# A quarter of one MLP weight chunk in each attention step: 32-row slices of a long PSUM sum in the idle row group

## The chip, the cores and the metric

One NeuronCore of one Trainium2 chip runs the whole program. The metric is the device time of that core in microseconds (us), the median of several executions. All executions that are compared here are fast, at a granted TensorE clock of 1.0 (0.998 in two executions).

Part of the scatter is the start of the program, which is the same in all versions: the 101st matmul with w1 starts between 28.60 and 29.19 us in the 14 profiles. Where a small difference matters, the text also gives the time from the start of that matmul to the end of the last matmul, called "without the start".

The engines have short names in the profile: PE is TensorE's matmuls, PEld its weight loads, DVE is VectorE, ACT is ScalarE, POOL is GpSimd, and SPq is the DMA queue that SyncE feeds. "Bank" is one of the eight parts in which the program uses PSUM; each holds the 512 float32 output columns of one matmul. An evacuation is the copy of finished results out of a bank, which frees the bank.

## The reference, cut to what matters

```python
x = A_x                                  # 2048 tokens x 1024
xn = layernorm(x)
return x + A(xn, wq, wk, wv, wo, beta) + B(xn, w1, b1, w2, b2)

# A: attention, 32 heads of 32, in 4 segments of 512 tokens: causal softmax
#    inside a segment, a linear-attention memory M, z over earlier segments
logits = einsum('bhqd,bhkd->bhqk', q_s, k_s) * scale + mask   # contraction over 32
p = softmax(logits); a_dot = p @ v_s; ...; o @ wo
# B: an MLP over the token axis, 3584 hidden units
u = gelu(einsum('bsd,sf->bdf', layernorm(xn), w1) + b1)
y = einsum('bdf,fs->bds', u, w2) + b2    # contraction over 3584 = 28 chunks of 128
```

Two kinds of work matter here. The logits contract over only 32 rows, so four heads share the 128-row array as four row groups: in the trace of the kernel before, the first four matmuls of a step in different row groups start 3 to 7 ns apart. The second MLP product contracts over 3584 rows: 32 output tiles (16 token chunks, two halves of 512 columns), each a sum of 28 full matmuls; 24 of them also add 8 matmuls of `o @ wo` to the same sum.

## The kernel before

The program is emitted by a small list scheduler. It emits attention tasks in order ("crit"), and between them it emits single matmuls of MLP output sums ("fill"), so that PE always has something to do. A logits step is one task. It takes seven banks: in a first round each of the four row groups streams 512 columns, in a second round three of them do. In the second round one row group, the "short" one, rotates with the step and has nothing to do.

```python
# _Kernel.step: items are (row group r, blocks); seven of them, four first
def mms(*bs):
    for i, u, r, kb, col in jobs:
        self.fw.mm(self.ps[:, bs[i], col:col + SEG_L - kb * P],
                   self.kT[u % 3][32*r:32*r+32, kb*P:(kb+1)*P],
                   self.qT[u % 3][32*r:32*r+32, kb*P:SEG_L],
                   start=True, stop=True, tile_position=(32*r, 0))
box = fl.pe(mms, reads, banks=len(slots), wall=True, ns=637)

# _Fill.step: one matmul of the current sum; the sum's bank stays taken meanwhile
st, sp = at == 0, at == size - 1
with fw.group(reads=reads, writes=[k.R_bank[b]] if st or sp else []):
    if at < N_FCH:                                     # 28 chunks of w2
        w, _ = k.w2_ring.get(4 * j + at // 7)          # 6 slots of 7 chunks
        fw.mm(k.bank(b), w[:, at % 7, :], k.gT[:, at, half*512:(half+1)*512],
              start=st, stop=sp)
    else:                                              # o @ wo, 8 more
        ...
# ... [cut: loads, projections, weighing, evacuation, the tail]
```

The two halves of a token chunk follow each other and use the same w2 slots, so each w2 chunk is loaded once.

## Time and profile before

| | before |
|---|---|
| time | 692.94 us (692.87 to 693.18) |
| PE busy | 687.3 of 691.2 us |
| 128-row matmuls with w2 | 896 |
| logits steps | 46, median 550.5 ns (541 to 559) |
| PE waits after the first 12 us | none |
| DMA moved | 77 MB, engines 44% busy |

A step's length is read from the single matmul records of the trace, from the start of its first matmul to the start of the next 128-row matmul. The page of the kernel before has these lines: busy time by engine, the DMA queue, the chain that ended last, the group of w2 matmuls (busy us, mean ns of one, idle before), and its loads (KB each, median us from issue to landing).

```profile
PE 687.3 (99%) x4822; PEld 329.7 (48%) x4822; DVE 260.3 (38%) x600; ACT 283.9 (41%) x516; POOL 145.1 (21%) x379
...
q1 hardware_dynamic: 211290, 76.59, 44.1%
...
PE 98%; ACT 1%; DMA 0%; DVE 0%; POOL 0%; issue 0%; SPq 0%; DVEq 0%
...
L217 PE MATMUL ps_all<-gT,w2h 128*128 128x512 bf16 x896 | 228.5, 379 | 0.0
...
w2h<-in_B_w_dram SPq DMA_DIRECT2D x64, 224.0 KB, 3.3
```

PE is the chain. A busy PE alone would not prove it, since the records of matmuls overlap: one lasts 379 ns (its end is modelled), while the records start 216 ns apart. So the next question is whether PE ever waits. The view of who PE waited for has one line:

```profile
PE ps_all L217 <- DVE gT L760: 1.3, 1, 1.3
```

That is the start of the program. The third view is one step in the timeline of PE (start us, us, then what ran):

```profile
411.64 0.38 PE L217 MATMUL ps_all<-gT,w2h 128*128 128x512 bf16 x1
411.96 0.61 PE L217 MATMUL ps_all<-qT,kT 32*128 32x512 bf16 x10
412.50 0.39 PE L217 MATMUL ps_all<-gT,w2h 128*128 128x512 bf16 x1
```

From 411.96 to 412.50 is the step. The last 128-row matmul started at 411.64, 0.32 us earlier instead of 0.216: about 0.1 us is lost on the way into the step. The trace shows 96 ns before each of the 46 steps (95 or 96 in all of them); what the engine does in that time is not shown.

### The profile page before, as it was taken

What the parts mean: (1) busy time and instruction counts of PE and PEld (TensorE: products, weight loads), DVE (VectorE), ACT (ScalarE), POOL (GpSimd) and SP (SyncE); (2) the same over time, 40 slices, a digit from 0 to 9 for tenths busy, and PEclk for the clock granted to TensorE, in tenths of its full rate; (3) what the DMA queues carried; (4) which work ended last, traced back from release to release, by engine and by line L of the source; (5) the groups of instructions that cost most, each with busy time, mean ns of one, the idle gap of its engine ahead of it and who ended that gap; (6) DMA issues with size and microseconds to landing.
All of it is one profiled execution on the core that took longest, in us unless ns stands there. A gap on an engine that the chain in (4) does not pass through costs nothing.

```text
span 691.2 us, 11771 instructions
## 1 busy us (share of the span) xinstructions
PE 687.3 (99%) x4822; PEld 329.7 (48%) x4822; DVE 260.3 (38%) x600; ACT 283.9 (41%) x516; POOL 145.1 (21%) x379
## 2 busy tenths in 40 slices
PE   9999999999999999999999999999999999999998
PEld 3444444444444544454454544444445444454454
DVE  6731100000002343344554564554545454353444
ACT  7331111111135455555455344455543435436420
POOL 5820000000001222223132122223221313214310
PEclk9999999999999999999999999999999999999999
DMA  8377666323027355444443526444452525242232
GB/s 309 119 180 183 155 157 206 94 61 101 1 102 194 69 120 133 103 117 114 101 113 75 128 46 131 96 104 102 99 128 60 111 62 123 68 108 70 52 99 83
DMA packets 211343, 77.33 MB, mean 112 GB/s; under 512 B 173915, under 2 KB 203611, under 8 KB 211291
## 3 DMA queue, kind: packets, MB, share of 16 engines
q1 hardware_dynamic: 211290, 76.59, 44.1%
q8 instruction: 38, 0.62, 0.4%
q14 instruction: 15, 0.11, 0.1%
HBM read 59.79 MB, written 5.24 MB: 94 GB/s over the span
## 4 chain that ended last, share of the span: by engine, by line
PE 98%; ACT 1%; DMA 0%; DVE 0%; POOL 0%; issue 0%; SPq 0%; DVEq 0%
PE ps_all L217 98%; ACT xn_tmp L809 0%; DMA xin<-in_A_x_dram 0%; ACT xn_tmp L811 0%; DVE h L850 0%; POOL ln_r L842 0%; SPq L245 0%; DVE fin L1292 0%; POOL ln_t L840 0%; DVE ln_mv L825 0%; DVEq L65 0%
## 5 line engine op out<-in xcount | busy, mean ns | idle before, releaser
L217 PE MATMUL ps_all<-gT,w2h 128*128 128x512 bf16 x896 | 228.5, 379 | 0.0
L1098 POOL TENSOR_SCALAR_AFFINE_SELECT pT<-pT 128x256 bf16<-128x256 bf16 (+1 forms) x320 | 118.8, 373 | 506.8 <-ACT pT L1090 493.9
L1090 ACT ACTIVATE pT<-ps_all 128x512 bf16<-128x512 f32 x320 | 161.8, 620 | 142.4 <-PE ps_all L217 142.2
L217 PE MATMUL ps_all<-h,w1all 128*128 128x512 bf16 x896 | 193.9, 379 | 0.2
L217 PEld LDWEIGHTS ps_all<-h,w1all 128*128 128x128 bf16 x896 | 87.5, 98 | 106.4 <-issue 0.8
L217 PEld LDWEIGHTS ps_all<-gT,w2h 128*128 128x128 bf16 x896 | 79.8, 97 | 85.2 <-issue 10.3
L964 ACT ACTIVATE gT<-ps_all,bc 128x512 bf16<-128x512 f32 x56 | 37.7, 689 | 140.6 <-PE ps_all L217 140.6
L1140 DVE CAST ost<-ps_all 128x264 bf16<-128x264 f32 (+1 forms) x128 | 50.0, 395 | 76.0 <-PE ps_all L217 75.8
L217 PEld LDWEIGHTS ps_all<-vA,pT 128*128 128x128 bf16 x1280 | 50.2, 96 | 28.8
L217 PE MATMUL ps_all<-xnT,wq 128*128 128x512 bf16 x256 | 60.5, 379 | 0.0
L217 PE MATMUL ps_all<-xnT,wk 128*128 128x512 bf16 x256 | 60.5, 379 | 0.0
L217 PE MATMUL ps_all<-wv_sb,xnT 128*128 128x512 bf16 x256 | 60.1, 379 | 0.0
L217 PE MATMUL ps_all<-vA,pT 128*128 128x33 bf16 x1280 | 51.5, 178 | 0.0
L902 DVE TENSOR_SCALAR gcol<-gcol 128x32 f32<-128x32 f32 x1 | 0.2, 183 | 118.7 <-ACT gcol L900 118.7
L217 PEld LDWEIGHTS ps_all<-wv_sb,xnT 128*128 128x128 bf16 x256 | 25.1, 98 | 30.2
L217 PEld LDWEIGHTS ps_all<-xnT,wk 128*128 128x128 bf16 x256 | 25.1, 98 | 30.2
L217 PEld LDWEIGHTS ps_all<-xnT,wq 128*128 128x128 bf16 x256 | 25.1, 98 | 30.2
L975 DVE TENSOR_SCALAR etmp<-etmp 128x512 bf16<-128x512 bf16 x48 | 14.1, 294 | 61.3 <-ACT etmp L974 61.3
L991 DVE CAST vA<-ps_all 128x512 bf16<-128x512 f32 x20 | 13.9, 694 | 56.7 <-PE ps_all L217 54.2
L217 PE MATMUL ps_all<-wo_sb,oT 128*128 128x512 bf16 x128 | 33.1, 379 | 0.0
L990 ACT ACTIVATE kT<-ps_all 128x512 bf16<-128x512 f32 x32 | 19.1, 597 | 34.1 <-PE ps_all L217 34.1
L991 DVE CAST qT<-ps_all 128x512 bf16<-128x512 f32 x20 | 13.8, 692 | 46.1 <-PE ps_all L217 46.1
(69 smaller groups left out, 427.2 us busy)
## 6 DMA issues: line engine op xcount, KB each, us to landing
w2h<-in_B_w_dram SPq DMA_DIRECT2D x64, 224.0 KB, 3.3
w1all<-in_B_w_dram SPq DMA_DIRECT2D x12, 1024.0 KB, 5.2
wq<-in_A_wq_dram SPq DMA_DIRECT2D x32, 256.0 KB, 3.0
wk<-in_A_wk_dram SPq DMA_DIRECT2D x32, 256.0 KB, 3.0
stg<-in_A_x_dram SPq DMA_DIRECT2D x16, 256.0 KB, 3.1
out_dram<-stg SPq DMA_DIRECT2D x16, 256.0 KB, 2.2
xin<-in_A_x_dram SPq DMA_DIRECT2D x5, 512.0 KB, 6.7
wv_sb<-in_A_wv_dram SPq DMA_DIRECT2D x2, 1024.0 KB, 8.3
```

What stands on the lines that cost most here:

```text
L217: ins = self.nc.tensor.matmul(out, *args, **kwargs)
L902: fw.op("dve", lambda e: e.tensor_scalar(self.gcol[:], self.gcol[:], 1.0, None, op0=ALU.add), reads=[self.R_gcol], writes=[self.R_gcol])
L964: fw.op("act", lambda e: e.activation(self.gT[:, fc, half * 512:(half + 1) * 512], self.bank(b), ACT.Gelu_apprx_tanh, bias=self.b1c[:, fc: ...
L975: fl.op({"dve": (lambda e: e.tensor_scalar(et[:], et[:], 1.0, None, op0=ALU.min), 294, 330)}, [R_et], [R_et], prio=2)
L990: self.flow.op({"act": (lambda e, b: e.activation(dst, view(self.bank(b)), ACT.Copy), 635, 560), "dve": (lambda e, b: e.tensor_copy(dst, v ...
L991: "dve": (lambda e, b: e.tensor_copy(dst, view(self.bank(b))), 690, 727)},
L1090: fl.op({"act": (lambda e, b, slot=slot: e.activation(pT[:, slot, :], self.bank(b), ACT.Exp, scale=SCALE), 620, 530)}, [], [R[slot]], box= ...
L1098: fl.op({"pool": (lambda e, ap=ap, pat=pat: e.affine_select(ap, ap, pattern=pat, compare_op=ALU.is_ge, fill=0.0, base=0, channel_multiplie ...
L1140: fl.op({"dve": (lambda e, b: e.tensor_copy(dst, self.ps[:, b, 0:n * VW]), 150 + n * 35, 185 + n * 35)}, [], [self.R_ost[o][qb]], box=box, ...
```

## The change

The intent: use the idle row group. A sum with 28 chunks needs 28 full matmuls of 216 ns. If its last chunk is cut into four slices of 32 rows, each slice is a matmul of 32 rows by 512 columns, and one of them fits into the idle row group of one step. The rotation of the idle group over four steps covers all four slices. The sum must then stay open over four steps, and its bank is the eighth: the other seven belong to the step. So all other sums must have ended before a step.

This costs more than one edit: two streams of sums ("L" for long ones, "N" for the ordinary ones) instead of one, each with its own weight slots; a step in two parts, the first of which needs four banks and the second the rest; and evacuations of attention results that may go to ACT as well as DVE. Eight of the nine long sums are cut. The core of the diff (the scheduler's pacing, buffer names and semaphore counts are cut):

```diff
@@ _Kernel.step
-        def mms(*bs):
-            for i, u, r, kb, col in jobs:
+        n = fl.stage - 1
+        rs = (3 - n) % 4                      # the short row group of this step
+        def mms(bs, some):
+            for i, u, r, kb, col in some:
                 ...
+        def second(bs, some):
+            if n >= fill.PLAIN and fill.L.sliced():
+                fill.L.cut(rs)
+            mms(bs, some)
+        def parts(bs):
+            k = min(4, len(bs))
+            one = sorted([j for j in jobs if j[0] < k], key=lambda j: j[4])
+            two = sorted([j for j in jobs if j[0] >= k], key=lambda j: j[4])
+            ...                               # two groups, each waits for its own banks
-        box = fl.pe(mms, reads, banks=len(slots), wall=True, ns=637)
+        box = fl.pe(None, reads, banks=len(slots), wall=True, parts=parts)
@@ _Kernel.weigh
-        fl.op({"dve": (... tensor_copy ...)},
+        fl.op({"dve": (... tensor_copy ...),
+               "act": (... activation Copy ...)},
@@ weights
-        self.w2r = [e.take(f"w2h{i}", [P, 7, P], BF16) for i in range(6)]
+        self.w2r = [e.take(f"w2n{i}", [P, 4, P], BF16) for i in range(6)]
+        self.w2l = [e.take(f"w2l{i}", [P, 6, P], BF16) for i in range(3)]
+        self.w2s = [e.take(f"w2s{i}", [P, P], BF16) for i in range(2)]
@@ _Stream
+    def cut(self, r):
+        k.fw.mm(k.bank(self.bank), k.w2s[self.i % 2][32*r:32*r+32, :],
+                k.gT[32*r:32*r+32, N_FCH - 1, half*512:(half+1)*512],
+                start=False, stop=False, tile_position=(32*r, 0))
@@ _Fill
+    PLAIN = 12                                # the first 12 steps carry no slice
+        self.L = _Stream(k, self, long, "L", k.w2l, k.R_w2l, 2, [3])
+        self.N = _Stream(k, self, rest, "N", k.w2r, k.R_w2, 4, [0, 1, 2])  # 4 slots ahead
+    def ready(self, t):                       # may this step start?
+        ...
+        return L.i == self.want(n) and L.open() and not self.N.open()
@@ _Flow.run
+    r = max([r, bs[-1]] if t.parts is None else [r, bs[3], bs[-1] - self.PART])
```

The two halves of a token chunk are now often in different sums or apart in time, so each half loads its own weights.

## The prediction

> **What bounds the kernel now.** TensorE. The busy table gives PE 687.3 of 691.2 us, the chain of waits puts 98% on PE, and the view of who waited for whom lists one PE wait (1.3 us, at the start). In the timeline a 128x512 matmul follows the last one after 216 ns; gaps above the ideal outside the logits steps sum to under 4 us, mostly the warm-up matmuls. The granted clock is 1.0. Only fewer or cheaper PE slots can help; ACT (284 us), DVE (260) and the DMA engines (44%) have room.
>
> A logits step (46 of them, 7 banks, 32-row matmuls in four row groups) takes about 550 ns from its first matmul to the next 128-row one, plus 96 ns lost just before it, against 0.43 us of streaming in two rounds of 512 columns. In the second round one row group is idle. [...]
>
> **What the change does.** By the instruction order, w2 matmuls of 128 rows fall from 896 to 888, and 32 matmuls of 32 rows by 512 columns are added, one in the second round of each of 32 steps, in the idle row group. Every other matmul count and the number of steps are equal.
> - Removed: 8 x 216 ns = 1.73 us of PE time, all on the critical path.
> - Added inside steps: 32 starts at 3 to 7 ns, 0.1 to 0.2 us. A slice is as long as the other columns of that round and should not lengthen it.
> - Loads: each half of an output chunk now loads its own weights, 206 loads of mostly 128 KB instead of 64 of 224 KB, about 14 MB more (77 to 91 MB). In 256-byte packets (18.4 ns each, 16 engines) that is about 65 us of DMA time: 44% becomes about 53%.
> - Prefetch of the ordinary sums: four slots of four matmuls, 16 x 216 ns = 3.5 us ahead. A weight load lands in 3.3 us (median), 4.2 us (90th percentile), and a transpose on the same queue holds the issue for 1.2 us. When such a sum runs 20 or more matmuls in one stretch, the fifth slot can come late. The order shows some six to ten such stretches; I estimate 0.3 to 1.2 us in all.
> - The long stream's sum holds the eighth bank through a step, so ordinary sums must have been evacuated (0.75 us DVE) before it. 56 of 128 attention evacuations go to ACT, which relieves this: 0 to 0.3 us.
>
> **Predicted time.** -1.73 + 0.15 + about 0.6 = -1.0 us: 691.9 us, 691.0 to 693.8 for 8 times in 10. Faster by over 2%: 0.004; within 2%: 0.99; slower: 0.006.
>
> **What would show it.** (1) Steps with a slice, timed from start to next 128-row matmul, still 540 to 565 ns; a serialised slice would add 100 to 200 ns each (3 to 6 us). (2) w2 groups count 888, 1.7 us less streaming. (3) New PE idle time, if any, released by DMA on the short weight tiles between 330 and 650 us; none by ACT or DVE over 0.3 us. (4) DMA share 52 to 55%.
>
> **What would make it wrong.** Slower: late weight loads at more places than I think, as loads collide on a busier queue; a slice that waits at the second round's start, or a second half whose banks come late. Faster than 691: no late loads and a shorter tail.

## The result, and the profile after

| | before | after |
|---|---|---|
| time, first comparison (6 runs each) | 692.95 us | 692.64 us (692.16 to 692.97) |
| time, second comparison (9 and 5 runs) | 692.94 us | 692.38 us (692.19 to 692.76) |
| ratio | | 0.9995 [0.9982, 1.0007], then 0.9991 [0.9979, 1.0004] |
| span of the profiled run | 691.2 us | 690.6 us |
| profiled run without the start | 660.00 us | 659.32 us, 659.44 in run 1 |
| steps, median | 550.5 ns | 545 ns, with or without a slice |
| DMA | 77 MB, 44% | 92 MB, 53.5% |

Ratios here are the mean time of one kernel's fast runs over the mean of the other's fast runs of the same rounds, so they are not quite the ratio of the medians quoted. By the medians the change is worth 0.3 to 0.6 us of 693. Both intervals include 1, so the times alone do not show a gain; the two profiles do, with 0.69 and 0.56 us without the start. Eight removed matmuls alone are 1.73 us. The question is where the other microsecond went.

The page after, with the lines that answer to those before:

```profile
PE 685.7 (99%) x4846; PEld 328.2 (48%) x4846; DVE 241.2 (35%) x545; ACT 299.7 (43%) x571; POOL 152.8 (22%) x379
...
q1 hardware_dynamic: 275642, 91.28, 53.5%
...
PE 97%; ACT 1%; DMA 1%; POOL 0%; DVE 0%; issue 0%; SPq 0%; POOLq 0%; DVEq 0%
...
L217 PE MATMUL ps_all<-gT,w2n 128*128 128x512 bf16 x644 | 151.3, 379 | 0.2 <-DMA w2n<-in_B_w_dram 0.2
...
L217 PE MATMUL ps_all<-gT,w2l 128*128 128x512 bf16 x244 | 63.7, 380 | 0.0
...
w2n<-in_B_w_dram SPq DMA_DIRECT2D x161, 128.0 KB, 2.8
```

644 + 244 = 888 matmuls of 128 rows, eight fewer. The slices are a group of their own in the list by shapes:

```profile
L217 PE MATMUL ps_all<-gT,w2s 32*128 32x512 bf16 x32 | 12.0, 374 | 0.0
```

PE waits, by whom (us in all, times, longest):

```profile
PE ps_all L217 <- DVE gT L800: 1.3, 1, 1.3
PE ps_all L217 <- DVE h L890: 0.7, 2, 0.5
PE ps_all L217 <- DMA w2n<-in_B_w_dram: 0.2, 1, 0.2
```

The first two are the start of the program (the second is missing in the next profile of the same kernel, that of run 1). The third is new. This view counts idle time only after the modelled end of the last matmul, which comes about 160 ns after the next one could have started (379 less 216), so it hides short waits. The distance between matmul starts shows them all. A step with a slice, in the timeline of PE:

```profile
397.32 0.38 PE L217 MATMUL ps_all<-wo_sb,oT 128*128 128x512 bf16 x1
397.63 0.39 PE L217 MATMUL ps_all<-qT,kT 32*128 32x384 bf16 x5
397.86 0.37 PE L217 MATMUL ps_all<-gT,w2s 32*128 32x512 bf16 x1
397.86 0.38 PE L217 MATMUL ps_all<-qT,kT 32*128 32x384 bf16 x6
398.18 0.39 PE L217 MATMUL ps_all<-wo_sb,oT 128*128 128x512 bf16 x1
```

The slice starts with the second round at 397.86, and the next 128-row matmul starts 0.55 us after the step's first: as long as a step without one.

I listed every start-to-start distance between 128-row matmuls after the first 15 us that was over 30 ns longer than the matmul needs, and every step that was too long. Before: none. After, in the first profile: six, 1.23 us in all. Three are late weight loads of ordinary sums (62 ns at 428 us, 377 ns at 602, 143 ns at 627: 0.58 us). Three are other waits (0.65 us). Here is a late load in the PE timeline, from the second profile of the changed kernel:

```profile
598.13 4.48 PE L217 MATMUL ps_all<-gT,w2n 128*128 128x512 bf16 x20
603.12 0.39 PE L217 MATMUL ps_all<-gT,w2n 128*128 128x512 bf16 x1 [0.51 <-DMA w2n<-in_B_w_dram]
```

Twenty matmuls are five slots of four. They run 216 ns apart, so the 21st could have started at 598.13 + 4.32 = 602.45 us. It starts at 603.12, 0.67 us late. By the code its slot is asked for when the sum is at its fifth matmul, 16 x 216 ns = 3.5 us ahead. In this trace the load was issued at 599.14 and landed 3.9 us later, at 603.07. In the first profile all three late loads are those of a sum's 21st matmul, and they landed 4.2, 3.6 and 3.8 us after their issue. Loads of 128 KB land in 2.8 us in the median and in up to 5.0 us.

The other three waits, each in the same place in every profile of this schedule, are in the unfiltered timeline of the first profile. At 368 us a step's second part waits for a bank that DVE (the update of the memory M) frees late:

```profile
368.33 0.29 DVE L1209 TENSOR_TENSOR MZ<-MZ,ps_all 128x132 f32<-128x132 f32 x1 [0.43 <-PE ps_all L217]
...
368.38 0.40 PE L217 MATMUL ps_all<-qT,kT 32*128 32x512 bf16 x4
...
368.77 0.37 PE L217 MATMUL ps_all<-gT,w2s 32*128 32x512 bf16 x1
```

The second round should have begun at 368.60 and began at 368.77. (The slice's own weights are a rival for this wait. The last load of such a weight before it was issued at 352.70 us, and the slowest of these loads in the profile took 2.4 us; the landing of this one is not in the trace.) At 444 us a projection waits for the first bank that ACT frees after a step. All eight banks were taken, seven by the step and one by the long sum that had just ended, which DVE starts to evacuate at 444.98:

```profile
444.25 1.09 ACT L1149 ACTIVATE pT<-ps_all 128x512 bf16<-128x512 f32 x2 [1.73 <-PE ps_all L217]
...
444.34 0.60 PE L217 MATMUL ps_all<-wo_sb,oT 128*128 128x512 bf16 x2
...
444.99 0.38 PE L217 MATMUL ps_all<-xnT,wq 128*128 128x512 bf16 x1
```

Two matmuls from 444.34 on end their streaming at 444.78. The first of the two ACT operations ends at 444.84, and the next matmul starts at 444.99. And at 671 us PE waits for a causal mask on POOL:

```profile
670.01 2.33 POOL L1157 TENSOR_SCALAR_AFFINE_SELECT pT<-pT 128x256 bf16<-128x256 bf16 x4
...
670.90 1.03 PE L217 MATMUL ps_all<-wo_sb,oT 128*128 128x512 bf16 x4
...
672.02 0.17 PEld L217 LDWEIGHTS ps_all<-vA,pT 128*128 128x128 bf16 x4 [0.60 <-POOL pT L1157]
```

The third of these four masks ends at 671.97, and the matmul that needs it starts at 672.03.

The balance of the first profile, from the end of the last matmul before (688.82 us) to after (688.15 us), a gain of 0.67 us:

| term | us |
|---|---|
| eight 128-row matmuls fewer, 8 x 216 ns | -1.73 |
| steps shorter, all 46 (25.33 to 25.26 us with the 0.18 below in it) | -0.24 |
| late w2 loads of ordinary sums, three | +0.58 |
| bank freed late by DVE (0.18) and by ACT (0.20), mask on POOL (0.27) | +0.65 |
| sum | -0.74 |

The sum is within 0.07 us of the gain. A balance of one trace is still only a reading, so its terms were tried on the chip. The exceptions are the mask at 671 us, which no run removes, and the waits at 368 and 444 us, which no run changes alone.

### The profile page after: what moved, and what is told of

Same layout as the page of the kernel before. It is cut to its first block, busy times and chain, and to the rows that moved or that the text cites. A ratio compares the mean times of both kernels' runs of the same rounds, so it can differ in the third digit from the quotient of the medians.

```text
span 690.6 us, 12093 instructions
## 1 busy us (share of the span) xinstructions
PE 685.7 (99%) x4846; PEld 328.2 (48%) x4846; DVE 241.2 (35%) x545; ACT 299.7 (43%) x571; POOL 152.8 (22%) x379
## 3 DMA queue, kind: packets, MB, share of 16 engines
q1 hardware_dynamic: 275642, 91.28, 53.5%
## 4 chain that ended last, share of the span: by engine, by line
PE 97%; ACT 1%; DMA 1%; POOL 0%; DVE 0%; issue 0%; SPq 0%; POOLq 0%; DVEq 0%
PE ps_all L217 97%; DMA w2n<-in_B_w_dram 1%; ACT xn_tmp L849 0%; DMA xin<-in_A_x_dram 0%; ACT xn_tmp L851 0%; POOL pT L1157 0%; DVE h L890 0%; ACT pT L1149 0%; POOL ln_r L882 0%; SPq L247 0%; POOLq L580 0%; DVE fin L1342 0%; POOL ln_t L880 0%; DVE ln_mv L865 0%; DVEq L65 0%
## 5 line engine op out<-in xcount | busy, mean ns | idle before, releaser
L1157 POOL TENSOR_SCALAR_AFFINE_SELECT pT<-pT 128x256 bf16<-128x256 bf16 (+1 forms) x320 | 126.4, 403 | 507.7 <-ACT pT L1149 497.5
L217 PE MATMUL ps_all<-gT,w2n 128*128 128x512 bf16 x644 | 151.3, 379 | 0.2 <-DMA w2n<-in_B_w_dram 0.2
L217 PEld LDWEIGHTS ps_all<-gT,w2n 128*128 128x128 bf16 x644 | 59.6, 98 | 68.4 <-issue 3.1
L217 PE MATMUL ps_all<-gT,w2l 128*128 128x512 bf16 x244 | 63.7, 380 | 0.0
L1462 DVE SCALAR_TENSOR_TENSOR stg<-ps_all,bc,stg 128x512 bf16<-128x512 f32 x32 | 24.0, 750 | 99.2 <-PE ps_all L217 99.1
L217 PEld LDWEIGHTS ps_all<-vA,pT 128*128 128x128 bf16 x1280 | 45.3, 96 | 15.5 <-POOL pT L1157 0.6
L217 PE MATMUL ps_all<-vA,pT 128*128 128x33 bf16 x1280 | 46.3, 177 | 0.1
L1200 ACT ACTIVATE ost<-ps_all 128x264 bf16<-128x264 f32 (+1 forms) x56 | 19.8, 366 | 58.2 <-PE ps_all L217 57.1
L1199 DVE CAST ost<-ps_all 128x264 bf16<-128x264 f32 (+1 forms) x72 | 28.0, 393 | 31.4 <-PE ps_all L217 31.1
L217 PEld LDWEIGHTS ps_all<-gT,w2l 128*128 128x128 bf16 x244 | 21.2, 97 | 24.9 <-issue 6.0
```

The source lines that it names most:

```text
L217: ins = self.nc.tensor.matmul(out, *args, **kwargs)
L1157: fl.op({"pool": (lambda e, ap=ap, pat=pat: e.affine_select(ap, ap, pattern=pat, compare_op=ALU.is_ge, fill=0.0, base=0, channel_multiplie ...
L1199: fl.op({"dve": (lambda e, b: e.tensor_copy(dst, self.ps[:, b, 0:n * VW]), 150 + n * 35, 185 + n * 35), "act": (lambda e, b: e.activation( ...
L1200: "act": (lambda e, b: e.activation(dst, self.ps[:, b, 0:n * VW], ACT.Copy), 230 + n * 27, 200 + n * 27)},
L1462: engs={"dve": (lambda e, b: e.scalar_tensor_tensor(dst, k.bank(b), k.b2c[:, c:c + 1], dst, op0=ALU.add, op1=ALU.add), 750, 785)},
```

## The experiments

Theory A: slices are free in the steps, and what is missing of the 1.73 us are PE waits (late loads first, then banks and a mask). Theory B: the slices cost most of it inside the steps. Within A, A1 says that the late loads are the larger part and can be removed; A2 says that they only hide bank waits, which would then show. Each run below has the kernel before beside it, on the same chip in the same rounds; "before" gives its median there. Runs 1 to 4, 5 to 8 and 9 to 12 are on three different chips. Unless it is said otherwise, an experiment edits the changed kernel and its result is correct.

**1. The changed kernel again** (before: 692.94).

> The changed kernel itself, as the base for the runs beside it on this chip. Theory A (slices are free in the steps; what is missing of the 1.73 us is PE waits: late w2 loads of the ordinary sums, some 0.6 us, and three waits for a bank or for a mask, some 0.65 us): 692.2 to 692.9 us, with waits at about the same places in a new profile. Theory B (the slices themselves cost most of the 1.73 us inside the steps): the same time, but steps with a slice would be longer than steps without by 20 ns or more.

Measured: 692.38 us. Its profile has 0.71 us of late loads (676 ns at 602 us, 36 ns at 428) and the same three other waits, 175, 204 and 273 ns. Steps with a slice last 545.5 ns in the median, without one 545.0. So the late loads move from execution to execution, and the other three waits stay. Whether the moving loads widen the spread of the changed kernel is not shown: it spreads over 0.57 us and the kernel before over 0.56.

**2. Whole chunks instead of slices**, in the same instruction order (the scheduler is told that the extra matmul costs nothing, so that it decides as before).

```diff
     def cut(self, r):
-        k.fw.mm(... 32-row slice r ...)
         self.cuts += 1
@@ _Stream.step, last matmul of a cut sum
+            if whole:
+                fw.mm(k.bank(b), k.w2s[self.i % 2][:], k.gT[:, N_FCH - 1, cols], start=False, stop=False)
+                fw._grp.cost = 0
```

> Same instruction order, but the four slices of a long sum are left out of the steps and its last chunk is one 128-row matmul at the end of the sum (8 in all). Right result. Theory A: 8 x 216 ns = 1.7 us slower than the changed kernel (1.5 to 1.9). Theory B: at most 0.9 us slower, since the steps get shorter again by what the slices cost.

Measured: 694.03 us, 1.65 us slower than the changed kernel in the same rounds. Steps last 545 ns without slices too. Theory B is out. The profile has no wait at 444 us: one of the eight whole matmuls starts at 444.75 us and fills the 0.20 us that the changed kernel waits there. Without the start, run 2 takes 660.85 us against 659.44 in run 1. To these 1.41 us belong 0.29 us that it waits less, which makes 1.70 us for the eight matmuls.

**3. No slices at all**: only the `k.fw.mm` in `cut` removed. One chunk of 28 is missing in 8 of 32 sums; the comparison with the reference did not notice. So "correct" in the other runs does not show that the slices are added rightly.

> Same instruction order, slices left out and nothing in their place; the result is wrong on purpose (8 of 32 sums lack one chunk). Theory A: 0 to 0.2 us faster than the changed kernel. Theory B: 0.8 us or more faster.

Measured: 692.16 us, 0.22 us faster than the changed kernel, which is less than either run's spread (0.68 and 0.57 us). Its profile has 0.15 us less of waits than run 1's (1.21 against 1.36 us, in different places). What is left for 32 slices is under 0.1 us, or about 2 ns each. The records of the steps say less still: without the late second part at 368 us, the 46 steps last 25.08 us here and 25.09 with slices.

**4. The slice in a busy row group.**

```diff
-                fill.L.cut(rs)
+                fill.L.cut((rs + 1) % 4)
```

> Same order and same count, but each slice goes to the next row group, which has 512 columns of its own in the second round (a sum's four steps still cover all four slices, so the result is right). Theory A, in which only the idle row group makes a slice free: each of 32 steps longer by about 216 ns, 6.9 us in all, minus waits that it hides: 5.5 to 7 us slower. If a slice were cheap for another reason[...]: under 3 us slower.

Measured: 698.3 us, 5.9 us slower. The timeline of PE shows one such step:

```profile
398.91 0.39 PE L217 MATMUL ps_all<-qT,kT 32*128 32x384 bf16 x5
399.14 0.38 PE L217 MATMUL ps_all<-gT,w2s 32*128 32x512 bf16 x1
399.14 0.59 PE L217 MATMUL ps_all<-qT,kT 32*128 32x384 bf16 x6
399.67 0.39 PE L217 MATMUL ps_all<-wo_sb,oT 128*128 128x512 bf16 x1
```

The step is now 757.5 ns in the median (751 to 909) instead of 545: the row group's own 384 columns start only after the slice, 215 ns later in the records of this step. 32 x 212 ns = 6.8 us. The late loads and the wait at 444 us are gone from this profile, and those at 368 (0.16 us, in the step of 909 ns) and 671 us (0.27) stay: 0.43 us of waits instead of 1.36. That the longer steps give the loads time is argued, not tested. So 6.8 less 0.9 is 5.9, as measured. A slice that costs at most about 2 ns in the idle row group (run 3) costs 212 ns in a busy one. The rival was that the 96 ns lost before each step hide a slice: they do not.

**5. Five slots ahead instead of four**, in the same six buffers (before: 692.97).

```diff
-        self.N = _Stream(k, self, rest, "N", k.w2r, k.R_w2, 4, [0, 1, 2])
+        self.N = _Stream(k, self, rest, "N", k.w2r, k.R_w2, 5, [0, 1, 2])
```

> One number changed: the ordinary sums prefetch five slots of w2 ahead instead of four (20 matmuls, 4.3 us, instead of 3.5 us; same buffers). The scheduler reorders a little for it. Theory A1 (late loads are the larger part of what is missing): no PE wait on the short weight tiles is left, 0.5 to 0.9 us faster than the changed kernel, 691.4 to 691.9 us. Rival A2 (the load waits only hide waits for banks, which then show): same as the changed kernel within 0.2 us.

Measured: 691.81 us (691.53 to 692.26), 1.16 us faster than before (ratio 0.9985 [0.9972, 0.9997]) and 0.6 to 0.8 faster than the changed kernel in its two comparisons. They were run at other times. Without the start it is 658.70 us against 659.32 and 659.44. In the profiles the order of instructions on PE, ACT, DVE and POOL is that of the changed kernel; only the order of the DMA issues differs. So this is a test of the prefetch alone. The timeline of PE has the whole sum in one piece, 28 matmuls without a wait:

```profile
598.07 6.21 PE L217 MATMUL ps_all<-gT,w2n 128*128 128x512 bf16 x28
604.11 0.59 PE L217 MATMUL ps_all<-wo_sb,oT 128*128 128x512 bf16 x2
```

No late load is left in its profile; the three other waits stay, at 176, 204 and 273 ns. A1 holds, A2 does not.

**6. The same bytes in larger pieces.** The ordinary sums' loads read 1 KB runs instead of 256 B runs, in the same instruction order on PE. The values are wrong (relative error 0.03).

```diff
-                rows = k.B_w2[f * P:e * P, c * P:(c + 1) * P] ... "(fc p) t -> p fc t"
+                k.B_w2[f * P:(f + 1) * P, q:q + 512] ... "p (fc t) -> p fc t"
```

> Exactly the changed kernel's instruction order; only the ordinary sums' weight loads read the same number of bytes in 1 KB pieces instead of 256 B pieces, so each load takes about 0.2 us less of the DMA engines. Values wrong on purpose. A1: late loads shrink or go, 0.3 to 0.6 us faster than the changed kernel; the waits at 368, 444 and 671 us stay. A2: same.

The 0.2 us of the expectation is an estimate that the first profile bears out: there a 256-byte packet took 18.2 ns on average and a 1 KB one 50.9, so 128 times four of the first against 128 of the second, on 16 engines, is 0.18 us.

Measured: 692.7 us, but from 691.93 to 693.53, the widest spread of all runs but 8. The loads landed in 2.66 us in the median. That is no clear gain: the two profiles of the changed kernel have 2.84 and 2.74, and run 5, with 256-byte pieces, has 2.59. The profile has 0.42 us of late loads in two places. The times decide nothing: this run is inconclusive, and why some of its executions were slow was not found.

**7. Three slots ahead.** The same line with 3.

> The opposite dose: three slots ahead (12 matmuls, 2.6 us), under the median landing time of 2.8 us. A1: late loads at more places, 1.5 to 3.5 us slower than the changed kernel. A2: under 0.5 us slower.

Measured: 695.52 us, 3.1 us slower than the changed kernel. PE waits, by whom:

```profile
PE ps_all L217 <- DMA w2n<-in_B_w_dram: 1.7, 4, 1.0
...
PE ps_all L217 <- ACT pT L1149: 0.2, 1, 0.2
```

By matmul distances the waits are 4.4 us in 14 places, about 2.9 us of them before a w2n matmul. The scheduler reorders here, unlike in run 5. The dose is in order: 3, 4 and 5 slots ahead give 695.5, 692.4 to 692.6 and 691.8 us.

**8. A step that waits for all its banks.**

```diff
-   r = max([r, bs[-1]] if t.parts is None else [r, bs[3], bs[-1] - self.PART])
+   r = max([r, bs[-1]])
```

> A logits step is started only when all its 7 banks are ready, instead of four with the rest 0.2 us later. If the split is what makes room for a long sum that holds the eighth bank: 4 to 11 us slower than the changed kernel, with many PE waits for banks. If the split is of no use: within 0.5 us.

Measured: 703.91 us (702.61 to 705.07, four executions), 11.3 to 11.5 us slower than the changed kernel, a little more than expected. Some of its lines of PE waits by whom:

```profile
PE ps_all L217 <- POOL pT L1157: 2.4, 3, 1.5
PE ps_all L217 <- ACT pT L1149: 2.0, 6, 0.6
PE ps_all L217 <- DMA w2n<-in_B_w_dram: 1.3, 4, 0.4
...
PE ps_all L217 <- DVE MZ L1209: 0.6, 1, 0.6
```

By distances 13.1 us are lost, among them seven steps whose second part comes 0.33 to 0.73 us late. About 1.4 of these 13.1 us are no waits: from 684.0 to 687.4 us the trace has a granted clock of 0.5, and six 512-column matmuls there are followed by the next only 426 ns after their start instead of 216, soon after a wait of 1.66 us at 681 us; why the clock was lower there is not shown. The scheduler's readiness rule for a split step is thus what makes an open long sum affordable in this schedule. The scheduler reorders here, so this is the whole effect of the rule, not of one wait.

**9. Only the order inside the steps**, in the kernel before (before: 692.86).

```diff
-            for i, u, r, kb, col in jobs:
+            for i, u, r, kb, col in sorted(jobs, key=lambda j: (j[0] >= 4, j[4])):
```

> The kernel before with one part of the change alone: the matmuls of a step are issued first round first, each round by column. Theory: this is what took the steps from 550 to 545 ns (median) in the changed kernel, so 46 x 5 ns = 0.25 us faster than before, and nothing else moves. Rival: the shorter steps come from the split of the wait; then the steps stay at 550 ns.

Measured: 692.58 us (692.49 to 692.61), 0.28 us faster than before, and 0.27 us faster without the start; steps 545 ns in the median instead of 550.5, their sum 25.07 instead of 25.33 us. That term of the balance belongs to the order of emission, not to the split.

**10. Five slots ahead with whole chunks**: edits 2 and 5 together.

> The deeper prefetch of the earlier run, but the slices as 8 whole matmuls again (right result). If the slices are the only gain of the change and the deeper prefetch only repairs what it broke: 1.6 to 1.8 us slower than the deeper prefetch with slices, 693.4 to 693.6 us, so not faster than the kernel before. If the new order of the sums helps by itself: under 692.7 us.

Measured: 693.06 us, 0.2 us slower than before. Its profile has the bank wait at 368 us (0.17) and the mask wait (0.27) and no late load: -0.24 for the shorter steps and +0.44 for these waits is +0.2. Without the start it is 660.20 us, 0.20 us slower than the kernel before too. So apart from the slices the reorganised kernel gains nothing, and the slices are worth 1.25 us here by the medians (1.36 by the differences to before, 1.65 in the same rounds in run 2, 1.50 without the start against run 5). The expectation of 1.6 to 1.8 us was too high: it left out that one of the eight whole matmuls fills the wait at 444 us (it starts at 444.83 here). Run 5 has that wait and this run has not. 1.73 less 0.20 is 1.53, near the 1.50. The medians say 0.15 to 0.25 us less, which is within their scatter.

**11. Five slots ahead, all attention evacuations on DVE.**

```diff
-        fl.op({"dve": (...), "act": (...)},
+        fl.op({"dve": (...)},
```

> The deeper prefetch, but all 128 attention evacuations on DVE as in the kernel before (the scheduler reorders). If the share given to ACT is needed to free banks in time: new PE waits for banks or masks, 0.5 to 2.5 us slower than the deeper prefetch (691.8). If it is not needed: within 0.3 us.

Measured: 694.32 us, 2.5 us slower than run 5. PE waits, by whom, without the program's start:

```profile
PE ps_all L217 <- ACT pT L1149: 1.5, 6, 0.3
...
PE ps_all L217 <- POOL pT L1157: 0.3, 1, 0.3
```

By distances 3.5 us of waits. Six of them, 0.20 to 0.43 us each, are the wait seen once at 444 us before: a projection's first matmul right after a step, while no bank is free. The share of evacuations given to ACT is needed.

**12. Five slots ahead with other pacing.** Scheduler numbers only.

```diff
-    MARGIN = 120, MARGIN_STEP = 80, RESERVE = 60, KEEP = 5, SOON = 600, 222 + 285 * s
+    MARGIN = 160, MARGIN_STEP = 120, RESERVE = 50, KEEP = 3, SOON = 900, 222 + 288 * s
     (and five slots ahead)
```

> The deeper prefetch with wider margins and other pacing numbers in the scheduler (a task counts as ready 160 instead of 120 ns after its inputs, a step 120 instead of 80; the close of an ordinary sum before a step is allowed from 3 instead of 5 matmuls). If the three remaining waits (0.65 us: a bank freed late by DVE at 368, by ACT at 444, a mask on POOL at 671 us) can be scheduled away: 691.2 to 691.6 us. If waits just move: 691.6 to 692.2.

Measured: 691.66 us (691.40 to 691.87), 1.2 us faster than before (ratio 0.9982 [0.9969, 0.9994]). The wait at 368 us is gone, those at 444 (204 ns) and 671 us (267 ns) stay. The time lies in the range expected for waits that just move. It is the fastest median and beats the kernel before; the changed kernel was not run beside it. Run 5 was within 0.15 us of it, so the two are not told apart.

## Why the prediction was right

The time (691.9 predicted, 692.64 and then 692.38 measured) lies in the stated range, and "within 2%" was right. The number alone tests little, since the range of 691.0 to 693.8 us also holds the time before, and there was some luck in it: two terms that were too low (banks and the mask) were partly cancelled by two that were too high or not foreseen (the slices' cost and the new order inside a step). What was right is the mechanism. Point by point:

- **PE bounds the kernel; only fewer slots help.** Right. Runs 2 and 10 put the matmuls back and lose 1.65 and about 1.3 us.
- **Removed: 8 x 216 ns = 1.73 us, all on the critical path.** Right by count and by run 2 (1.65), but for one matmul: without it PE waits 0.20 us for a bank at 444 us.
- **A slice adds 3 to 7 ns and does not lengthen the round.** The 3 to 7 ns are the distances of starts in different row groups in the trace of the kernel before. The mechanism was right (run 4 shows the counterpart, 212 ns a step, where the prediction's 100 to 200 ns for a serialised slice was an estimate), the size was too high: about 2 ns each at most (run 3), since a slice starts with the others of its round, 226 to 240 ns into the step (31 of 32; the other is the late one at 368 us), and ends with them.
- **Late loads, 0.3 to 1.2 us at six to ten places.** The sum was right (0.58 and 0.71 us), the places were too many (three and two), so that the agreement of the sum is partly luck. The prediction named the fifth slot; it is the sixth, because by the code slots 1 to 5 are asked for while the sum is not yet running, and slot 6 when it reaches its fifth matmul.
- **Banks: 0 to 0.3 us, none by ACT or DVE over 0.3.** This is the term that was mis-sized. DVE 0.18 and ACT 0.20 are 0.38 us, and a mask on POOL adds 0.27, which was not thought of. The predicted sum held nothing for either. These 0.65 us, less the 0.24 of the next point and the 0.15 foreseen for the slices, make the gain in the balance 0.74 us instead of the predicted 1.0. By the medians the result is 0.5 to 0.7 us behind the predicted one. The rest of that, 0.2 to 0.4 us, is of the size of the scatter, and no profile explains it. And "relieves this" was too weak for the evacuations on ACT: without them 2.5 us are lost (run 11).
- **Not foreseen:** the new order inside a step takes 5 ns off each of 46 steps, 0.24 us (run 9).
- **DMA 52 to 55%.** Right, 53.5%.

What stays open: why the loads of run 6 did not help in its times, and whether the waits at 444 and 671 us can be scheduled away, since run 12 removed only the one at 368; and whether the slices' values are right, which the comparison cannot tell.

## What to carry to other kernels

Here an idle row group was worth nearly the matmuls that it took over (1.65 of 1.73 us in run 2), and a 32-row slice there cost at most about 2 ns where the group was idle for its whole length; the price is a bank that stays taken, and waits for banks that the kernel before does not have (0.18 us for DVE and 0.20 for ACT in the first profile). When such a change splits one weight stream into several smaller ones, recompute the prefetch distance in time (matmuls ahead x 216 ns here) against the slow landings and not the median: 3.5 us against 2.8 in the median and 5.0 at worst cost 0.6 us, and one more slot in the same buffers gave it back. In a trace of a full PE, look for waits by the distance between matmul starts, because the view of idle time does not count waits shorter than the tail of a matmul's record (379 less 216, about 160 ns here).

## What else the traces show

- In the trace of the kernel before, a matmul that waits for its own row group does not hold up the next group. The step at 230.89 us, which the program holds in the order 384, 128 (row group 0), 384, 128 (row group 1), 512, 512, ... columns, starts at 0 (384), 7 (384), 13 (512), 17 (512) and only then 173 and 179 ns (the two 128s). Sorting the emission was worth only 5 ns a step (run 9).
- The first starts of a step in different row groups are 3 to 4 ns apart where the program goes on to another group with each matmul (all 138 distances in the first profile of the changed kernel), and up to 7 ns where the program alternates within a group (kernel before).
- Beside a step, PE loses 96 ns before it (46 of 46 within 2 ns) and about 90 ns after it: in the 41 steps of the first profile of the changed kernel that have a 512-column matmul in the second round, the next 128-row matmul starts 306 to 332 ns after the last of these, while 512-column matmuls of 128 rows follow each other after 216.
- In run 6 a 256-byte packet took 18.3 ns and a 1 KB one 54.4 ns on average over all loads and stores, so four of the first take 1.35 times one of the second. The landing times of whole loads showed no clear gain (2.66 us in run 6, 2.59 to 2.84 in three profiles with 256-byte pieces).
- On the DMA queue of these runs, with other loads around, 128 KB in 256-byte pieces landed in 2.2, 2.8 and 5.0 us (least, median, most, in the first profile of the changed kernel). A prefetch distance needs this spread: it was 3.5 us here.
